# Attention with a gated mixer on one core: shifted keys copied within SBUF instead of computed by products

## The chip, the cores and the metric

The kernel runs on one core of a Trainium2 chip. The metric is the device time of one execution in microseconds, as a median of several runs. The profile is one further execution, taken by the hardware profiler; its span, and all times within it, count from the first instruction.

## What is computed

The input `x` is 2048 tokens by 512, in bf16. Path A is attention with 32 query heads of width 16 that share one head of keys and values. Path B is a gated MLP whose gate mixes along the tokens. A sigmoid per token mixes the two.

```python
g = sigmoid((x * gate_w).sum(-1))
q = (x @ wq) as 32 heads of 16;  k = x @ wk;  v = x @ wv
a = softmax(q k^T / 4) v, heads joined, @ wo
z = gelu(x @ w_in)            # 2048 x 1376
z1, z2 = halves of z;  z2 = layernorm(z2)
b = (z1 * (w_sp @ z2 + b_sp)) @ w_out
out = g * a + (1 - g) * b
```

## The kernel before

**Units.** The attention is cut into 32 units: a chunk of 512 queries (4 of them) times 4 heads (8 groups of them). A unit needs its scores against 16 tiles of 128 keys, for each of the 4 heads: 64 blocks of 128 keys by 512 queries. A score block is one product of the TensorE (PE) with 32 contracted rows: `ps<-QA,KA` in the rows of the trace. The 4 heads of a unit take the 4 groups of 32 rows. A group holds two heads of 16 rows, so that two units share one query tile `QA`: the even unit multiplies by keys that stand in rows 0 to 15 of each group with zeros below (`KA[:,0,:]`, "K0"), the odd unit by the same keys in rows 16 to 31 with zeros above (`KA[:,1,:]`, "K1", the shifted keys).

**Two ways to the exponential.** Most blocks go to the ScalarE (ACT): one activation for 2 blocks (1024 columns), sometimes 3 (1536) or 1 (512), writes `P` (line L770). The others go to the VectorE (DVE) in batches of 4 blocks (one key tile): a linear step from PSUM into `UW` (L782), a square (L789) and a second square (L795, of which GpSimd (POOL) takes a part). The products with the values, `ps<-P,V`, `ps<-UW,V` and `ps<-UW,VW`, and two small ones of sums (`ps<-QA,KTV`, `ps<-CT,SVB`) end the unit.

**Fillers.** Between these the PE does the products of path B, of queries and of the output projections. Everything on the PE but score blocks goes through the helper at L354.

**The planner.** The order is not written out. While the kernel is built, a planner keeps a clock for PE, ACT and DVE with a modelled cost per instruction, and emits the next instruction of the engine that is free first. How many batches the DVE gets, and how many blocks an activation takes, follow from it. Its constants stand at the head of the file: `A_OV` is the modelled fixed cost of an activation, `FLEX` bounds the DVE's backlog below which the third bank of an activation step goes to the DVE, `WARM` counts the products of a constant tile `CT` ahead of all others (L353). When the PE would idle after 20 us of planned time, it emits **zero products** (`ps<-CT,zer`) that add zeros or write an unused bank.

**The head.** The transposed loads of `x` come in four chunks of 512 tokens in the order 0, 3, 2, 1 (`XO`, on SyncE's (SP's) queue). For each chunk the PE makes K0 (`g_K`: 4 contraction steps of 4 products, 16 rows `ps<-xT,wk_rep`), then V (`ps<-wvg,xT`). The DVE evacuates K0 into `KA` (L426). After V of the last chunk come the products of **K1**, again 16 per chunk, from a second copy of the weights placed in the tile `z1` (`ps<-xT,z` in the rows, where buffer numbers are left out), and again a DVE evacuation at L426. A batch of an odd unit needs K1 of chunk 3. SP's queue goes on in order: `win` (L297), `bspz`, `wo`, `wout`, then `wT`.

**The end.** After the last unit the DVE normalizes and transposes in two halves (L807 to L838); 16 products `ps<-wo,OT` finish four output tiles of 128 tokens, numbers 12 to 15. The DVE evacuates 12 and 13 (L697), ACT 15 and 14 (L728). SP stores 12, 13 and 14, ACT stores 15.

Of the kernel before, what the change touches and what calls it, by code (L numbers as in the profile page):

```python
# [7 lines left out]
ALU = mybir.AluOpType  # L8
# [8 lines left out]
DH = 16  # L17
# [4 lines left out]
NU = 32  # L22
# [18 lines left out]
NZ = 22  # L41
WARM = 12
RLAST = 16
XO = (0, 3, 2, 1)
N0 = 3
A_OV = 63.3
HEAD = 45000.0
# [8 lines left out]
W_GEL = 0.98  # L56
PR = dict(HALF=100.0, IDR=10, IDN=4, WRES=16, D_HG=2500.0, D_FL=False, WIN=1000.0, WIH=560.0, BACK=32, PRESS=5, FLEX=5000.0, RMIN=32, WBL=0.5, W_MIN=0.9, HOLD=0.0, RLEND=0)
SCHED = {}
# [108 lines left out]
def build_kernel(nc, x_d, wq_d, wk_d, wv_d, wo_d, win_d, wsp_d, bsp_d, wout_d, gw_d, out_d):  # L167
    es = ExitStack()
    with es:
# [75 lines left out]
        SF = tmp[:, 64 * NMAX:96 * NMAX].rearrange("p (k w) -> p k w", w=32)  # L245
        wk_r = [wk_rep[:], z1f[:, 512 * NZ - 512:512 * NZ].rearrange("p (a n) -> p a n", a=4)]
        PT = z2[:, 0:2048].bitcast(F32).rearrange("p (a n) -> p a n", a=2)
# [6 lines left out]
        op("dve", lambda v: v.memset(CT[:], 1.0 / 64.0), w=["CT"])  # L254
        for e in range(2):
            op("dve", lambda v, e=e: v.memset(wk_r[e], 0.0), w=[("wk_rep", e)])
# [37 lines left out]
        op("act", lambda q: q.dma_start(wvg[:, :, 0:DH], wv_d.rearrange("(dt p) d -> p dt d", p=128)), w=["wv"], dma=16)  # L294
        op("act", nonc(lambda q: q.dma_start(wvg[:, :, 2 * DH:2 * DH + 1], gw_d.rearrange("(dt p one) -> p dt one", p=128, one=1))), w=["gw"], dma=16)
        def ld_win():
# [21 lines left out]
        def ld_rest():  # L318
            ld_bsp(0)
            sp_dma(ld_wo, w=["wo"], n=128)  # L320
# [5 lines left out]
        for e in range(2):  # L326
            op("dve", lambda v, e=e: v.tensor_scalar(wk_r[e].rearrange("p a (g e d) -> p a g e d", e=2, d=DH)[:, :, :, e, :],
                                                     wk_sb[:].unsqueeze(2).broadcast_to([128, 4, 4, DH]), 0.25, None, ALU.mult),
               r=["wk"], w=[("wk_rep", e)])

# [30 lines left out]

        ld_win()
        ld_rest()
        for _ in range(WARM):
# [53 lines left out]

        def g_K(c, lo=0, hi=512, e=0, b=BM):
            key = "K0a" if c == XO[0] and lo == 0 and e == 0 else ("K%d" % e, c)  # L420

            def piece(dt):
                return lambda: fm(b, hi - lo, 0, wk_r[e][:, dt, :], xT[:, dt, 512 * c + lo:512 * c + hi], dt == 0, dt == 3, [("wk_rep", e), ("x", c), ("z1", 5)], "K")

            def ev():
                op("dve", lambda v: v.tensor_copy(KA[:, e, 512 * c + lo:512 * c + hi], bank(b, hi - lo)), r=[bkey(b)], w=[key], tag="Kev")  # L426

            def done(t):
                T[key] = t
                if e == 0 and all(("K0", c2) in T for c2 in range(4)) and hi == 512:  # L430
# [465 lines left out]
        for i, c in enumerate(XO):  # L896
# [5 lines left out]
        first = deque([g_K(XO[0], 0, 128), g_Q(0, DBK[0]), g_K(XO[0], 128, 512), g_V(XO[0], BO), g_K(XO[1]), g_V(XO[1], BO), g_K(XO[2]), g_V(XO[2]),  # L902
                       g_K(XO[3]), g_V(XO[3])] + [g_K(c, e=1) for c in (XO[1], XO[0], XO[2], XO[3])])
        early = deque()
# [12 lines left out]
        tails = deque([g_part(12), g_part(13), g_flag(),  # L917
                       g_out(14, BM, None, True, "sp"),
                       g_out(15, DBK[0], lambda: d_done(), True, "act"),
                       g_fin(12, EB[0][0], lambda: when(("Bend", 0)), "sp"),  # L920
# [315 lines left out]
        pbusy = deque()  # L1236
        pidle = [0]

        def pe_step(now):
            r = pe_work(now)  # L1240
            if r is None:
# [3 lines left out]
                u = st_["pu"]  # L1245
                if now > 20000.0 and b < (W_GEL if gst["arm"] and gst["t"] > now - 8000.0 else pr["W_MIN"]) * W_WIN:
                    lim, topen = limit(now)
# [464 lines left out]
        if INFO is not None:  # L1712
            print({"end": last_end, "busy": busy, "batches": len(batches), "hist": hist, "left": left, "sbuf": nc.sbuf_bytes_remaining})
            print("warm", pidle[0])
            INFO.update(T=T, units=units, estart=estart, stepb=stepb, busy=busy, log=log)
        if INFO is not None and st_["pu"] < NU:
# [177 lines left out]
```

## Time and profile before

| what | value |
|---|---|
| median of 3 runs | 729.82 us (729.63 to 729.87) |
| the profiled execution, its own time | 732.05 us |
| its span | 730.2 us |
| granted TensorE clock, mean of the span | 0.993 |
| busy: PE, DVE, ACT, POOL | 714.8, 704.5, 711.9, 466.9 us |
| exponentials on ACT | 741 |
| score blocks that go through the DVE | 552 |

A row of a timeline has start and duration in us, engine, line, operation, tiles out<-in, shapes and the count; in square brackets how long the engine sat idle ahead of it, and what ended that. A row of the stretches has the busy time of PE, weight loads, DVE, ACT and POOL, then the granted clock of the PE (1.00 is full speed), the share of the DMA engines, and GB/s. A row of the groups by shape has the count, the busy time in us, the mean ns of one, and the idle time ahead of them. A row of the waits has who waited for whom, us in total, times, and the longest. A row of the DMAs ends in the us from issue to landing.

### The profile page before, as it was taken

To read this page: it belongs to the slowest core of one execution; us is meant where nothing else is said; L and a number is where in the kernel's file an instruction comes from. 1 tells how busy PE (TensorE), PEld (TensorE's weight loads), DVE (VectorE), ACT (ScalarE), POOL (GpSimd) and SP (SyncE) were. 2 spreads that over 40 slices of the span, in tenths; PEclk is the share of its full clock that TensorE was granted. 3 is DMA by queue.
4 is the path that set the end of the run, shared out by engine and by line. 5 is a ranking of instruction groups with operands and counts; after the bars stand their busy time and mean duration, and the time that the engine had idled before them with its cause. 6 is when DMAs were issued, how large, how long until landed. Compare 5 with 4: busy or idle time off the path is not lost.

```text
span 730.2 us, 21786 instructions
## 1 busy us (share of the span) xinstructions
PE 714.8 (98%) x9037; PEld 208.4 (29%) x9037; DVE 704.5 (96%) x1035; ACT 711.9 (98%) x760; POOL 466.9 (64%) x437
## 2 busy tenths in 40 slices
PE   8999999999999999999999999999999999999996
PEld 3322333323422223222222222222232222222321
DVE  5799999999999999999999999999999999999995
ACT  4999999999999999999999999999999999999996
POOL 5643666662166778776677777767776567667661
PEclk8999999999999999999999999999999999999999
DMA  8340000000000000500000051000005100000000
GB/s 189 110 108 10 2 1 2 2 3 2 2 2 1 2 2 2 116 24 9 1 2 2 3 103 36 10 2 1 3 2 105 27 10 9 1 3 2 2 2 33
DMA packets 48608, 17.28 MB, mean 24 GB/s; under 512 B 44180, under 2 KB 47992, under 8 KB 48504
## 3 DMA queue, kind: packets, MB, share of 16 engines
q1 hardware_dynamic: 46248, 15.54, 9.4%
q8 instruction: 72, 1.18, 0.6%
q10 hardware_dynamic: 2256, 0.30, 0.3%
q14 instruction: 32, 0.26, 0.1%
HBM read 3.25 MB, written 2.10 MB: 7 GB/s over the span
## 4 chain that ended last, share of the span: by engine, by line
PE 69%; ACT 17%; DVE 9%; issue 5%; ACTq 0%; DVEq 0%
PE ps L354 69%; ACT P L770 15%; DVE UW L782 4%; DVE UW L789 1%; DVE UW L795 1%; PE ps L353 1%; ACT z L1327 1%; DVE z L584 1%; DVE bst L598 0%; ACT z L592 0%; DVE T L807 0%; DVE km L453 0%; DVE KA L426 0%; DVE QA L471 0%; ACT outsb L728 0%
## 5 line engine op out<-in xcount | busy, mean ns | idle before, releaser
L770 ACT ACTIVATE P<-ps 128x1024 bf16<-128x1024 f32 (+1 forms) x741 | 686.6, 1177 | 7.8 <-PE ps L354 7.5
L795 POOL TENSOR_TENSOR UW<-UW 128x512 f16<-128x512 f16 (+1 forms) x281 | 363.5, 1294 | 161.2 <-DVE UW L795 67.4
L782 DVE TENSOR_SCALAR UW<-ps 128x512 f16<-128x512 f32 (+1 forms) x424 | 347.0, 840 | 4.1 <-PE ps L354 3.1
L354 PE MATMUL ps<-QA,KA 32*128 32x512 bf16 x2048 | 312.8, 386 | 6.1 <-ACT P L770 2.9
L354 PE MATMUL ps<-P,V 128*32 128x512 bf16 x1496 | 212.9, 387 | 0.3 <-DVE KN L499 0.2
L354 PEld LDWEIGHTS ps<-QA,KA 32*128 32x128 bf16 x2048 | 84.5, 91 | 309.7 <-ACT P L770 152.8
L789 DVE TENSOR_TENSOR UW<-UW 128x2048 f16<-128x2048 f16 (+1 forms) x163 | 171.8, 1056 | 0.6
L354 PE MATMUL ps<-UW,VW 128*32 128x512 f16 x552 | 118.9, 384 | 0.0
L354 PE MATMUL ps<-wT,z 128*32 128x512 bf16 (+1 forms) x1536 | 116.2, 366 | 0.0
L795 DVE TENSOR_TENSOR UW<-UW 128x1024 f16<-128x1024 f16 (+5 forms) x167 | 108.4, 664 | 0.2
L354 PE MATMUL ps<-UW,V 128*32 128x512 f16 x552 | 84.4, 384 | 0.2 <-DVE T L807 0.2
L354 PEld LDWEIGHTS ps<-P,V 128*32 128x32 bf16 x1496 | 49.0, 94 | 57.0 <-issue 51.1
L475 POOL TENSOR_TENSOR QSQ<-QA 128x512 bf16<-128x512 bf16 x16 | 28.9, 1806 | 22.9 <-DVE z L612 7.0
L354 PEld LDWEIGHTS ps<-wT,z 128*32 128x32 bf16 x1536 | 27.7, 94 | 42.5 <-issue 41.9
L354 PEld LDWEIGHTS ps<-UW,VW 128*32 128x32 bf16 x552 | 28.1, 94 | 15.0 <-issue 11.6
L354 PE MATMUL ps<-wout,z 128*32 128x512 bf16 x384 | 31.6, 384 | 0.0
L354 PE MATMUL ps<-win,xT 128*32 128x344 bf16 x512 | 30.8, 312 | 0.1
L830 POOL TENSOR_TENSOR Tn<-T,rc 128x512 bf16<-128x512 f32 x15 | 24.6, 1638 | 6.4 <-DVE UW L782 3.1
L807 DVE STREAM_TRANSPOSE T<-ps 128x512 f32<-128x512 f32 (+1 forms) x33 | 22.7, 691 | 4.1 <-PE ps L354 4.1
L354 PE MATMUL ps<-QA,KTV 128*32 128x512 bf16 x128 | 25.0, 384 | 0.0
L354 PE MATMUL ps<-CT,SVB 128*32 128x512 bf16 x128 | 24.6, 384 | 0.0
L354 PEld LDWEIGHTS ps<-UW,V 128*32 128x32 bf16 x552 | 20.0, 94 | 15.6 <-issue 11.3
(116 smaller groups left out, 380.1 us busy)
## 6 DMA issues: line engine op xcount, KB each, us to landing
out_dram<-outsb SPq DMA_DIRECT2D x15, 128.0 KB, 1.7
win<-in_B_w_in_dram SPq DMA_DIRECT2D x1, 1376.0 KB, 6.0
wout<-in_B_w_out_dram SPq DMA_DIRECT2D x1, 640.0 KB, 4.8
wo<-in_A_wo_dram SPq DMA_DIRECT2D x8, 64.0 KB, 2.3
UW<-in_A_wq_dram SPq DMA_DIRECT2D x1, 384.0 KB, 4.0
wT<-in_B_w_sp_dram SPq DMA_TRANSPOSE x16, 4.6
UW<-in_A_wq_dram ACTq DMA_DIRECT2D x1, 128.0 KB, 3.9
out_dram<-outsb ACTq DMA_DIRECT2D x1, 128.0 KB, 2.7
```

The costliest lines, as they stand in the source:

```text
L353: return t.matmul(dst, lhsT, rhs, start=start, stop=stop)
L354: return t.matmul(dst, lhsT, rhs, start=start, stop=stop, tile_position=tp)
L475: dq(pl_q, 1050.0, lambda: op("pool", lambda v: v.tensor_tensor(QSQ[:, q % 2, :], QA[:, q % NQ, :], QA[:, q % NQ, :], ALU.mult), r=[("Q", ...
L584: ev = lambda: op("dve", lambda v: v.tensor_copy(z2[:, FH * st + 344 * h:FH * st + 344 * h + 344], bank(BM, 344)), r=[bkey(BM)], w=[("z2", ...
L770: op("act", lambda a: a.activation(P[:, 512 * p0:512 * (p0 + n)], ps[:, 512 * b0:512 * (b0 + n)], ACT.Exp), r=[bkey(b0 + i_) for i_ in ran ...
L782: op("dve", lambda v: v.tensor_scalar(UW[:, 0, s, 512 * i:512 * (i + n)], bank(b, 512 * n), Q_A, Q_AS, ALU.mult, ALU.add), r=[bkey(b + j) ...
L789: op("dve", lambda v: v.tensor_tensor(src, src, src, ALU.mult), r=k, w=k, tag="dTT")
L795: op(eng, lambda v: v.tensor_tensor(UW[:, 1, s, 256 * a:256 * b], src, src, ALU.mult), r=[("U", s, h) for h in range(a // 2, (b + 1) // 2) ...
L807: return lambda: pgx.op("dve", lambda v: v.transpose(T1[:, jj, c0:c1], bank(BO, c1 - c0, c0)), r=[bkey(BO)], w=[("T1", jj, c0)], tag="T1")
L830: pgx.op(eng, lambda v: v.tensor_tensor(tnv[:, pr, j0:j1, b0:b1, :], t1v[:, j0:j1, b0:b1, 0:16], rc[:, j0:j1, b0:b1].unsqueeze(3).broadcas ...
L1327: op("act", lambda a: a.activation(z1f[:, 512 * i0:512 * (i0 + n)], ps[:, 512 * b0:512 * (b0 + n)], ACT.Gelu_apprx_tanh), r=[bkey(b0 + j) ...
```

## The change

The products and evacuations of K1 go, with the second copy of the weights. Instead SP copies, per chunk, rows 0 to 111 of K0 into rows 16 to 127 of K1: 112 rows of 1 KB, once the chunk's K0 is evacuated. The zeros that this leaves out (rows 0 to 15 of the first group) are written by POOL at the start. On SP's queue the copies of chunks 3, 0 and 2 stand ahead of `win`, that of chunk 1 ahead of `bspz` and what follows. `WARM` goes from 12 to 11. After the last product of the last unit the planner emits zero products for 1850 ns. Tile 14 is stored by ACT, tile 15 by SP. `A_OV` and `FLEX` are lower. `W_HEAD` has the value that stood in the code before, and the factor 1.0 beside it is for planned times below 20 us, which that value excludes.

```diff
-WARM = 12
+WARM = 11
+W_HEAD = 20000.0
+W_TAIL = 1850.0
-A_OV = 63.3
+A_OV = 62.9
-PR = dict(... FLEX=5000.0 ...)
+PR = dict(... FLEX=3500.0 ...)
+op("pool", lambda g: g.memset(KA[0:32, 1, :], 0.0), w=[("K1", c) for c in range(4)])
+def ld_K1(c, t):
+    op("sp", lambda q: q.dma_start(KA[16:128, 1, 512*c:512*c+512], KA[0:112, 0, 512*c:512*c+512]),
+       r=[("K0", c)] + (["K0a"] if c == XO[0] else []), w=[("K1", c)], dma=16, tag="K1")
+    spc["free"] = max(spc["free"], t) + 650.0
+    T[("K1", c)] = spc["free"] + 2300.0
 # in g_K, when the evacuation of chunk c is planned:
+if hi == 512 and c == XO[1]:
+    ld_K1(c, t)
+    ld_K1(XO[0], t)
+elif hi == 512 and c == XO[2]:
+    ld_K1(c, t)
+    ld_win()
+elif hi == 512 and c == XO[3]:
+    ld_K1(c, t)
+    ld_bsp(0)
+    sp_dma(ld_wo, w=["wo"], n=128)
+    ld_rest()
-first = deque([...] + [g_K(c, e=1) for c in (XO[1], XO[0], XO[2], XO[3])])
+first = deque([...])
-g_out(14, BM, None, True, "sp"), g_out(15, DBK[0], lambda: d_done(), True, "act"),
+g_out(14, BM, None, True, "act"), g_out(15, DBK[0], lambda: d_done(), True, "sp"),
 # in pe_step, when the PE has nothing to do:
+if u >= NU and tend[0] is not None and now + C_V <= tend[0] + W_TAIL:
+    fm(EB[1][0] + 1, 512, 0, zer[:], CT[:], True, True, ["zer", "CT"], "warm")
-elif now > 20000.0 and b < (W_GEL if ... else pr["W_MIN"]) * W_WIN:
+elif now > W_HEAD and b < (1.0 if now < 20000.0 else W_GEL if ... else pr["W_MIN"]) * W_WIN:
```

**What moves on SP, at the head of its queue.** Before, `win` follows the loads of `x`:

```order
L287 DMA_TRANSPOSE xT<-in_A_x_dram 128x4x512 x2
L291 DMA UW<-in_A_wq_dram 128x4x384
L287 DMA_TRANSPOSE xT<-in_A_x_dram 128x4x512 x2
L297 DMA win<-in_B_w_in_dram 128x4x1376
L300 DMA bspz<-in_B_b_sp_dram 1x512
L306 DMA wo<-in_A_wo_dram 16x4x512 x8
```

With the change the four copies stand among them:

```order
L288 DMA_TRANSPOSE xT<-in_A_x_dram 128x4x512 x2
L292 DMA UW<-in_A_wq_dram 128x4x384
L288 DMA_TRANSPOSE xT<-in_A_x_dram 128x4x512 x2
L300 DMA KA<-KA 112x512 x3
L306 DMA win<-in_B_w_in_dram 128x4x1376
L300 DMA KA<-KA 112x512
L309 DMA bspz<-in_B_b_sp_dram 1x512
L315 DMA wo<-in_A_wo_dram 16x4x512 x8
```

So `win` now waits on this queue for K0 of the third chunk, and all that follows for K0 of the fourth.

**What moves on the DVE, around the evacuation of the fourth chunk's K0** (the first `KA` row of each piece). Before, from the evacuation of the sums to the third evacuation of K1:

```order
L550 TENSOR_SCALAR z<-ps 128x512
L795 TENSOR_TENSOR UW<-UW 128x1024 x2
L426 CAST KA<-ps 128x512
L492 CAST V<-ps 128x4x16
L495 TENSOR_SCALAR gs<-ps 128x4
L570 TENSOR_SCALAR G<-E 128x16
L571 RECIPROCAL G<-G 128x16
L426 CAST KA<-ps 128x512
L782 TENSOR_SCALAR UW<-ps 128x512
L426 CAST KA<-ps 128x512
L782 TENSOR_SCALAR UW<-ps 128x512 x2
```

With the change, from the same place:

```order
L565 TENSOR_SCALAR z<-ps 128x512
L797 TENSOR_SCALAR UW<-ps 128x1024
L810 TENSOR_TENSOR UW<-UW 128x1024 x2
L797 TENSOR_SCALAR UW<-ps 128x512
L430 CAST KA<-ps 128x512
L797 TENSOR_SCALAR UW<-ps 128x512 x2
L804 TENSOR_TENSOR UW<-UW 128x2048
L507 CAST V<-ps 128x4x16
L510 TENSOR_SCALAR gs<-ps 128x4
L797 TENSOR_SCALAR UW<-ps 128x1024
L585 TENSOR_SCALAR G<-E 128x16
L586 RECIPROCAL G<-G 128x16
```

The work on batches of the odd unit 1 (`UW` rows) now stands ahead of and around the last evacuation of K0, where before the DVE had only small evacuations. Over the whole program ACT gets 738 exponentials with 1492 blocks, where it had 741 with 1496: 718 of 1024 columns (725 before), 18 of 1536 (15), 2 of 512 (1). The DVE gets 139 batches, where it had 138. Ahead of path B's gelu, ACT now has 332 blocks in 163 exponentials (347 in 171 before), behind it 1160 in 575 (1149 in 570); the DVE has 115 blocks ahead of it and 441 behind (116 and 436).

**What moves on ACT and the PE at the end.** ACT before, from its last exponentials on:

```order
L770 ACTIVATE P<-ps 128x1536
L770 ACTIVATE P<-ps 128x1024 x2
L728 ACTIVATE outsb<-ps,G 128x512
L662 DMA out_dram<-outsb 128x512
L728 ACTIVATE outsb<-ps,G 128x512
```

With the change:

```order
L785 ACTIVATE P<-ps 128x1024
L785 ACTIVATE P<-ps 128x1536
L785 ACTIVATE P<-ps 128x1024
L743 ACTIVATE outsb<-ps,G 128x512 x2
L677 DMA out_dram<-outsb 128x512
```

The PE before, from the last unit's sums on:

```order
L354 MATMUL ps<-QA,KTV 32x512 x4
L354 MATMUL ps<-P,V 32x512 x2
L354 MATMUL ps<-CT,SVB 32x512 x4
L354 MATMUL ps<-UW,VW 32x512 x4
L354 MATMUL ps<-P,V 32x512 x2
L354 MATMUL ps<-wo,OT 32x512 x16
```

With the change:

```order
L360 MATMUL ps<-QA,KTV 32x512 x4
L360 MATMUL ps<-CT,SVB 32x512 x4
L360 MATMUL ps<-P,V 32x512 x2
L360 MATMUL ps<-CT,zer 32x512 x32
L360 MATMUL ps<-wo,OT 32x512 x16
```

ACT's two evacuations now follow each other, with its store behind both, and 32 zero products stand between the last unit and the output projection.

More of the change, by code (lines that the diff above doesn't have):

```diff
@@ L56 @@
 W_GEL = 0.98
[L57 removed]
+PR = dict(HALF=100.0, IDR=10, IDN=4, WRES=16, D_HG=2500.0, D_FL=False, WIN=1000.0, WIH=560.0, BACK=32, PRESS=5, FLEX=3500.0, RMIN=32, WBL=0.5, W_MIN=0.9, HOLD=0.0, RLEND=0)
 SCHED = {}
@@ L254, in build_kernel @@
         op("dve", lambda v: v.memset(CT[:], 1.0 / 64.0), w=["CT"])
-        for e in range(2):
-            op("dve", lambda v, e=e: v.memset(wk_r[e], 0.0), w=[("wk_rep", e)])
+        op("dve", lambda v: v.memset(wk_rep[:], 0.0), w=["wk_rep"])
         op("dve", lambda v: v.memset(V1[:], 0.0), w=[("V", c) for c in range(4)])
@@ L324, in ld_rest @@
             ld_wT(0)
[L326 to L329, printed above, removed]
+        op("dve", lambda v: v.tensor_scalar(wk_rep[:].rearrange("p a (g e d) -> p a g e d", e=2, d=DH)[:, :, :, 0, :],
+                                            wk_sb[:].unsqueeze(2).broadcast_to([128, 4, 4, DH]), 0.25, None, ALU.mult),
+           r=["wk"], w=["wk_rep"])
         def wq_tile(eng, t, key, raw):
@@ L417, in qt, with g_K @@
             return 1e12 if t is None else t
-        def g_K(c, lo=0, hi=512, e=0, b=BM):
-            key = "K0a" if c == XO[0] and lo == 0 and e == 0 else ("K%d" % e, c)
+        def g_K(c, lo=0, hi=512, b=BM):
+            key = "K0a" if c == XO[0] and lo == 0 else ("K0", c)
             def piece(dt):
-                return lambda: fm(b, hi - lo, 0, wk_r[e][:, dt, :], xT[:, dt, 512 * c + lo:512 * c + hi], dt == 0, dt == 3, [("wk_rep", e), ("x", c), ("z1", 5)], "K")
+                return lambda: fm(b, hi - lo, 0, wk_rep[:, dt, :], xT[:, dt, 512 * c + lo:512 * c + hi], dt == 0, dt == 3, ["wk_rep", ("x", c)], "K")
             def ev():
-                op("dve", lambda v: v.tensor_copy(KA[:, e, 512 * c + lo:512 * c + hi], bank(b, hi - lo)), r=[bkey(b)], w=[key], tag="Kev")
+                op("dve", lambda v: v.tensor_copy(KA[:, 0, 512 * c + lo:512 * c + hi], bank(b, hi - lo)), r=[bkey(b)], w=[key], tag="Kev")
             def done(t):
                 T[key] = t
-                if e == 0 and all(("K0", c2) in T for c2 in range(4)) and hi == 512:
+                if hi == 512 and c == XO[1]:
[9 more added lines that the diff above has]
+                    ld_rest()
+                if all(("K0", c2) in T for c2 in range(4)) and hi == 512:
                     for c2 in range(4):
@@ L902, in build_kernel @@
         first = deque([g_K(XO[0], 0, 128), g_Q(0, DBK[0]), g_K(XO[0], 128, 512), g_V(XO[0], BO), g_K(XO[1]), g_V(XO[1], BO), g_K(XO[2]), g_V(XO[2]),
-                       g_K(XO[3]), g_V(XO[3])] + [g_K(c, e=1) for c in (XO[1], XO[0], XO[2], XO[3])])
+                       g_K(XO[3]), g_V(XO[3])])
         early = deque()
@@ L1152, in pv_emit @@
                 st_["pu"] += 1
+                if st_["pu"] == NU:
+                    tend[0] = t_end
                 unit_end(pu, t_end + L_PE)
@@ L1237, in build_kernel @@
         pidle = [0]
+        tend = [None]
         def pe_step(now):
@@ L1245, in pe_step @@
                 u = st_["pu"]
-                if now > 20000.0 and b < (W_GEL if gst["arm"] and gst["t"] > now - 8000.0 else pr["W_MIN"]) * W_WIN:
+                if u >= NU and tend[0] is not None and now + C_V <= tend[0] + W_TAIL:
+                    fm(EB[1][0] + 1, 512, 0, zer[:], CT[:], True, True, ["zer", "CT"], "warm")
+                    pidle[0] += 1
+                    r = now + C_V
+                elif now > W_HEAD and b < (1.0 if now < 20000.0 else W_GEL if gst["arm"] and gst["t"] > now - 8000.0 else pr["W_MIN"]) * W_WIN:
                     lim, topen = limit(now)
@@ L1714, in build_kernel @@
             print("warm", pidle[0])
-            INFO.update(T=T, units=units, estart=estart, stepb=stepb, busy=busy, log=log)
+            INFO.update(pg=pg, T=T, units=units, estart=estart, stepb=stepb, busy=busy, log=log)
         if INFO is not None and st_["pu"] < NU:
```

11 lines of the change are left out of this document (4 added, 7 removed).

## The prediction

> **What bounds the kernel now.** I read the busy times first, then stretches of the span, then ACT's waits.
>
> ```profile
> PE 714.8 (98%) x9037; PEld 208.4 (29%) x9037; DVE 704.5 (96%) x1035; ACT 711.9 (98%) x760; POOL 466.9 (64%) x437
> ```
>
> Three engines are nearly full, so the average doesn't name the bound. The stretches do: from the head's end to the gelu, from behind the gelu to the end of the attention, and the tail.
>
> ```profile
> 9.70:21.00 11.30, 10.29 (x197) 2.79 (x190) 6.46 (x14) 9.46 (x10) 6.09 (x13) 0.70 0.83 204
> 21.00:171.00 150.00, 146.78 (x1957) 45.45 (x1949) 145.82 (x205) 149.87 (x163) 94.29 (x100) 1.00 0.10 25
> 195.00:720.00 525.00, 523.38 (x6344) 144.84 (x6334) 520.59 (x728) 524.59 (x569) 360.94 (x301) 1.00 0.08 17
> 720.00:730.20 10.20, 3.20 (x43) 0.87 (x38) 3.71 (x12) 3.18 (x4) 0.00 (x0) 0.86 0.17 57
> ```
>
> ACT (fourth busy time) idles 0.13 of 150 us and 0.41 of 525 us; the DVE (third) 4.2 and 4.4. In the whole span ACT waits for the PE's scores for 7.5 us, of which 5.5 are the start:
>
> ```profile
> ACT P L770 <- PE ps L354: 7.5, 6, 5.5
> ```
>
> So the time is ACT's work, plus the head, plus the tail. The DVE binds as strongly only if work is moved to it without room. The room lies in the head:
>
> ```profile
> 20.00:40.00 20.00, 19.92 (x406) 7.04 (x402) 15.39 (x30) 19.51 (x21) 15.32 (x35) 0.98 0.30 82
> ```
>
> 4.6 us of DVE idle time stand here, most of them where it has no batch because unit 1's keys are not there:
>
> ```profile
> 27.95 0.69 DVE L426 CAST KA<-ps 128x512 bf16<-128x512 f32 x1 [0.68 <-PE ps L354]
> ...
> 31.54 0.69 DVE L426 CAST KA<-ps 128x512 bf16<-128x512 f32 x1 [0.95 <-PE ps L354]
> 33.26 0.69 DVE L782 TENSOR_SCALAR UW<-ps 128x512 f16<-128x512 f32 x1 [1.02 <-PE ps L354]
> ```
>
> The last K0 is evacuated at 27.95, the first K1 at 31.54, and the first batch of unit 1 begins at 33.26.
>
> **Part 1: K1 by copy, and the batch that it pays for: -1.9 us.** ACT's price of a block and of an instruction:
>
> ```profile
> L770 ACT ACTIVATE P<-ps 128x1024 bf16<-128x1024 f32 x725 | 668.0, 1171 | 2.0 <-PE ps L354 1.7
> ...
> L1327 ACT ACTIVATE z<-ps 128x1536 bf16<-128x1536 f32 x3 | 4.3, 1447 | 0.2 <-PE ps L354 0.2
> L1327 ACT ACTIVATE z<-ps 128x1024 bf16<-128x1024 f32 x4 | 4.1, 1016 | 0.1
> ```
>
> One of 1024 columns costs 668.0/725 = 0.921 us of ACT's time (its own 1171 ns overlap with the next); 512 columns more cost 1.447 - 1.016 = 0.431. The order gives 7 fewer of 1024, 3 more of 1536 (1.352) and 1 more of 512 (0.490): -6.45 + 4.06 + 0.49 = **-1.9 us**. I take all of it, since ACT has no idle time in which to lose it unnoticed.
>
> It holds only if the DVE carries its side.
>
> ```profile
> L782 DVE TENSOR_SCALAR UW<-ps 128x512 f16<-128x512 f32 x296 | 191.6, 678 | 3.6 <-PE ps L354 3.0
> L782 DVE TENSOR_SCALAR UW<-ps 128x1024 f16<-128x1024 f32 x128 | 155.4, 1214 | 0.5 <-PE ps L354 0.2
> L789 DVE TENSOR_TENSOR UW<-UW 128x2048 f16<-128x2048 f16 x113 | 138.1, 1222 | 0.6
> L795 DVE TENSOR_TENSOR UW<-UW 128x1024 f16<-128x1024 f16 x113 | 76.3, 685 | 0.1
> ```
>
> Linear steps: 14 more of 1024 (1.21), 24 fewer of 512 (0.65): +1.5. Squares: the order holds 4608 columns more in 9 more instructions; from 1.22 for 2048 and 0.68 for 1024 a column costs 0.53 ns and an instruction 0.13 us: +3.6. Four evacuations of 0.69 go: -2.8 (the second copy of the weights goes too, unpriced). Sum +2.3, where the span is to shrink by 2.4: 4.7 of the DVE's 25.7 idle us (730.2 - 704.5) must go, and unit 1's batches now stand where the 4.6 above lie.
>
> The split at the gelu agrees: ahead of it ACT has 15 blocks in 8 instructions fewer (at 0.43, and the 0.06 that 0.921 leaves for an instruction: -6.9 us), behind it 11 in 5 more (+5.0). The gelu's table load should move from 171.6 to near 164.5:
>
> ```profile
> 171.56 1.28 ACT L592 ACT_TABLE_LOAD   x1
> ```
>
> The copy itself must not be late. Chunk 3's waits for the evacuation at 12.10; like transfers land after about 2 us:
>
> ```profile
> 12.10 0.69 DVE L426 CAST KA<-ps 128x512 bf16<-128x512 f32 x1 [1.94 <-PE ps L354]
> ```
> ```profile
> wo<-in_A_wo_dram SPq DMA_DIRECT2D x8, 64.0 KB, 2.3
> ```
>
> So it lands at 12.8 + 2.3 = 15.1 us, or near 19 if it takes as long as `win`, 6.0 (below). The order has unit 1's first score (a 3 in place of a 2) here:
>
> ```profile
> 22.76 0.39 PE L354 MATMUL ps<-QA,KA 32*128 32x512 bf16 x2
> ```
>
> The cover is 7.7 us, so I cost the copy at nothing. Later than 22.76, it would hold the PE, and all scores for ACT queued behind it.
>
> Behind it on SP, `win` is held until K0 of chunk 2 stands, at 19.4, and lands 6 us later, near 26; its first reader on the PE stands behind the last K0 (evacuated at 27.95), V and a query tile. The weights behind the fourth copy wait for that evacuation and are read after the gelu. POOL's zeros lie ahead of a gap of 5.03 us in which it waits for `wq`, and cost nothing up to that:
>
> ```profile
> 18.72 0.69 DVE L426 CAST KA<-ps 128x512 bf16<-128x512 f32 x1 [0.38 <-PE ps L354]
> ```
> ```profile
> win<-in_B_w_in_dram SPq DMA_DIRECT2D x1, 1376.0 KB, 6.0
> ```
> ```profile
> 9.79 1.32 POOL L333 COPY wqd<-UW 128x256 bf16<-128x256 bf16 x3 [5.03 <-DMA UW<-in_A_wq_dram]
> ```
>
> The PE loses 64 products (16 groups of four at 0.22 us, 3.5 us) which were covered by ACT; that gives nothing by itself.
>
> **Part 2: one warm product fewer: -0.2 us.**
>
> ```profile
> 1.44 5.30 PE L353 MATMUL ps<-CT 128*128 128x512 bf16 x12 [1.44 <-DVE CT L254]
> 6.67 0.59 PE L354 MATMUL ps<-xT,wk_rep 128*32 128x128 bf16 x16
> 7.07 1.06 PE L354 MATMUL ps<-xT,wqd 128*32 128x512 bf16 x16
> ```
> ```profile
> 0.72 4.96 SPq L287 DMA_TRANSPOSE xT<-in_A_x_dram  x2
> ```
> ```profile
> xT<-in_A_x_dram SPq DMA_TRANSPOSE x1, 5.2
> ```
>
> The first load of `x` is issued at 0.72 and lands at 5.9; the first K0 starts at 6.67, right behind the 12 products of 0.43 us each. One fewer frees 0.43 us. But these are half-speed products (0.43, where groups of four from 7.07 on take 0.22). If full speed comes at the same instant, the query products start in the slow part and give back about half. Bounds 0 and -0.43; I take -0.2.
>
> **Part 3: the end: -0.3 us.**
>
> ```profile
> 725.21 0.69 ACT L728 ACTIVATE outsb<-ps,G 128x512 bf16<-128x512 f32 x1 [3.40 <-PE ps L354]
> 725.93 0.37 ACTq L662 DMA_DIRECT2D out_dram<-outsb  x1
> 726.40 0.69 ACT L728 ACTIVATE outsb<-ps,G 128x512 bf16<-128x512 f32 x1 [0.50 <-ACT outsb L728]
> ```
> ```profile
> 727.11 0.42 SPq L662 DMA_DIRECT2D out_dram<-outsb  x1
> ```
> ```profile
> out_dram<-outsb SPq DMA_DIRECT2D x1, 128.0 KB, 2.4
> ```
> ```profile
> out_dram<-outsb ACTq DMA_DIRECT2D x1, 128.0 KB, 2.7
> ```
>
> ACT's store sits between its two evacuations. Without it the second starts at 725.9, and the last store is issued at 726.6, not 727.11. It lands 2.4 to 2.7 us later: -0.2 to -0.5. I take -0.3, nearer to ACT's own 2.7. The zero products (8 groups, 1.8 us) fall into the PE's wait here:
>
> ```profile
> 724.32 1.05 PE L354 MATMUL ps<-wo,OT 128*32 128x512 bf16 x16 [2.07 <-DVE OT L838]
> ```
>
> 1.8 is less than 2.07, and the 16 products already run at 0.22 a group, so they gain and cost nothing. The cover has 0.3 us to spare; what it falls short of would be added to the end.
>
> **Sum.** -1.9 - 0.2 - 0.3 = -2.4 us. The profiled execution took 732.05 (span 730.2 and 1.85 around it), 2.2 above the median; the difference carries over: 732.05 to 729.65, or 729.82 to **727.4 us**.
>
> **Rivals.**
> *The DVE doesn't keep up ahead of the gelu.* There ACT's time falls by 6.9 us, and the DVE's work by 3.5 (the four evacuations, and one block at about 0.7): it must do with 3.4 us less idle time, most of what it has from 20 to 40. If the idle time stays, the batch's 1.9 go and only 0.5 remain: 729.3. For it: no reserve. Against: DVE work now stands in those gaps.
>
> *The new order feeds ACT later, slower than before.* 23 exponentials take 21.18 us in a quiet stretch, which is (21.18 - 1.17)/22 = 0.909 each; the mean of all is 0.921. So 12 ns each are waits for scores. The mechanism is the PE's order behind the gelu, where other things now stand ahead of the scores. If these waits double, that is 738 x 0.012 = 8.9 us: 736.3. It eats the gain from 3 ns each on, and is slower than before by more than 0.2% from 5 ns on. Against: behind the gelu ACT and DVE both have 11 and 5 blocks more, at the mix of before.
>
> ```profile
> 59.61 21.18 ACT L770 ACTIVATE P<-ps 128x1024 bf16<-128x1024 f32 x23
> ```
>
> *The half-speed stretch goes away.* Inside the stretch from 9.7 to 21 us, with its mean of 0.70, the PE falls to half clock (the granted clock stands ahead of the last two numbers):
>
> ```profile
> 14.00:15.00 1.00, 1.00 (x9) 0.10 (x2) 0.97 (x2) 1.00 (x2) 0.89 (x3) 0.50 0.21 44
> ```
>
> ACT idles 1.84 of 11.3 us there (9.46 busy). The head now runs 0.2 us earlier, which packs more work ahead of the drop. If the drop then fails to come, 1.8 more are won: 725.6. Against: the order up to 22 us is the same.
> The Trainium skill, TensorE: Matmul & The Clock Gate, "Part 1: The HAM clock gate", says the clock falls after at least one idle window of about 3.4 us. By that rule there would be no drop here to lose, and the sum stays 727.4; the trace disagrees, since the PE was busy 10.29 of 11.30 us and still fell to half.
>
> *The change doesn't do what it says*, the copies being unused until later: the DVE's order excludes it.
>
> **How the numbers follow.** Forecast 0.64 (own range 726.4 to 728.8), DVE short of room 0.20, slower 0.08, half-speed gone 0.08. A measurement of this kernel can tell about 0.2%, 1.46 us, from no change. Faster: 0.08 and most of the forecast, 0.56; same: 0.20 and the rest, 0.08; slower 0.08. The range takes in 725.6 and 729.3 with some margin for the sizes: 725.5 to 729.9.
>
> **What will show it.** Right: 738 exponentials; ACT idle under 1 us between 21 us and the end of attention; DVE busy over 18.5 us from 20 to 40; the table load near 164.5; the copies landing by 17 us; the first K0 near 6.3 us; the last store at a distance of 1.4 us, not 1.9, from ACT's first evacuation. Wrong: DVE gaps ended by the PE ahead of the gelu, a mean exponential over 0.924, or PE rows waiting for `KA`'s copies.

## The result, and the profile after

The changed kernel takes **731.68 us** (median of 9 runs, 731.53 to 732.5), the kernel before 729.94 beside it (9 runs): a ratio of 1.0023, with a 95% interval of 1.0012 to 1.0033. It is slower by 1.7 us, where 2.4 us less were forecast.

One thing about the ground of the comparison: the stretch at half clock in the first profile of before (14 to 20.8 us) is missing in most executions (of the nine of before, eight take 729.63 to 730.25 us and one, like that profile, 732.06), so from here on before is read in a second profile, with a span of 727.9 us, and after in one of 730.0. The gap to close is thus **+2.1 us** of span.

The busy times of after:

```profile
PE 709.3 (97%) x9004; PEld 207.4 (28%) x9004; DVE 711.0 (97%) x1028; ACT 710.7 (97%) x757; POOL 471.9 (65%) x439
```

DVE rose by 6.5 us, where the sum had 2.3. The stretches say where it matters; second profile of before first (busy PE, weight loads, DVE, ACT, POOL, then the clock), then after:

```profile
14.00:15.00 1.00, 0.64 (x9) 0.10 (x2) 0.97 (x2) 1.00 (x3) 0.89 (x3) 1.00 0.95 213
20.00:40.00 20.00, 19.91 (x351) 6.62 (x349) 16.16 (x27) 20.00 (x22) 16.85 (x38) 1.00 0.33 97
40.00:60.00 20.00, 19.06 (x210) 5.28 (x208) 20.00 (x25) 19.87 (x22) 6.15 (x6) 1.00 0.43 93
```
```profile
20.00:40.00 20.00, 18.61 (x330) 6.26 (x323) 19.96 (x29) 18.95 (x23) 16.98 (x38) 1.00 0.40 135
40.00:60.00 20.00, 18.47 (x217) 5.25 (x217) 20.00 (x25) 18.52 (x20) 6.92 (x6) 1.00 0.39 86
21.00:171.00 150.00, 144.60 (x1929) 45.67 (x1926) 148.41 (x203) 147.45 (x157) 89.46 (x96) 1.00 0.12 33
```

Before, ACT was busy 39.87 of these 40 us; after, 37.47. The PE, too, has less to do. The DVE's row says 19.96 of 20 while the other two starve. ACT's waits for scores, before (second profile) and after (in all these rows the scores, too, have the line of the helper, L354 and now L360):

```profile
ACT P L770 <- PE ps L354: 5.8, 2, 5.5
```
```profile
ACT P L785 <- PE ps L360: 8.3, 10, 5.3
```

Two waits became ten. Each costs more than its gap: from the start at 44.07 to that at 45.52 us (rows below) it is 1.45 us, 0.54 more than in a row, around a gap of 0.43. So I count the distance from one start to the next. Where nothing waits it is 0.904 to 0.921 us for 1024 columns and 1.330 to 1.348 for 1536; I take 0.908 and 1.335, and by the same step 0.48 for 512 columns, which no row shows in a run of them. What exceeds this I call **lost time**. Over all exponentials that start from 20 to 60 us it is 0.8 us before and 4.1 after. The span's +2.1 is then: the first exponential 0.2 earlier (9.74 to 9.54); ACT's smaller work -1.9 (the same distances, over the exponentials and evacuations of each trace); lost time from 20 to 60 us **+3.3**; lost time elsewhere and ACT's other work +0.6; and 0.3 more from the last exponential to the end (8.40 to 8.69).

What fills the DVE from 40 to 46 us of after; DVE, POOL, PE and ACT:

```profile
40.19 1.20 DVE L797 TENSOR_SCALAR UW<-ps 128x1024 f16<-128x1024 f32 x1
41.32 1.91 DVE L804 TENSOR_TENSOR UW<-UW 128x2048 f16<-128x2048 f16 x1
43.16 1.52 DVE L810 TENSOR_TENSOR UW<-UW 128x1024 f16<-128x1024 f16 x1
44.60 0.68 DVE L468 TENSOR_REDUCE km<-ps 128x1 f32<-128x512 f32 x1
45.20 1.21 DVE L797 TENSOR_SCALAR UW<-ps 128x1024 f16<-128x1024 f32 x1
```
```profile
41.11 1.04 POOL L490 TENSOR_TENSOR QSQ<-QA 128x512 bf16<-128x512 bf16 x1
42.94 1.19 POOL L452 TENSOR_TENSOR KSQ<-KA 128x512 bf16<-128x512 bf16 x1 [0.79 <-PE ps L360]
```
```profile
43.29 0.39 PE L360 MATMUL ps<-UW,V 128*32 128x512 f16 x1 [0.37 <-DVE UW L804]
...
46.47 0.40 PE L360 MATMUL ps<-QA,KA 32*128 32x512 bf16 x4 [0.47 <-DVE UW L797]
```
```profile
39.87 3.77 ACT L785 ACTIVATE P<-ps 128x1024 bf16<-128x1024 f32 x4
44.07 1.02 ACT L785 ACTIVATE P<-ps 128x1024 bf16<-128x1024 f32 x1 [0.43 <-PE ps L360]
45.52 1.02 ACT L785 ACTIVATE P<-ps 128x1024 bf16<-128x1024 f32 x1 [0.43 <-PE ps L360]
46.99 1.02 ACT L785 ACTIVATE P<-ps 128x1024 bf16<-128x1024 f32 x1 [0.45 <-PE ps L360]
```

Two squares last 1.91 and 1.52 us that elsewhere take 1.22 and 0.68. Each begins while POOL is at an instruction and ends a fixed time behind it: QSQ ends at 42.15, the square of 2048 columns at 43.23, 1.08 later; KSQ ends at 44.13, the square of 1024 at 44.68, 0.55 later. The linear step at 40.19, which reads PSUM, is not touched by POOL; of the 133 steps of 1024 columns in after that begin beside a POOL instruction, none lasts over 1.23 us. The step at 45.20, which frees a PSUM bank, is so much later; the PE's scores wait for that bank (46.47), and ACT for the scores. The Trainium skill, SBUF — State Buffer, "SBUF: two separate sides", says that VectorE and GpSimd share a pair of ports which one instruction holds to its end while the other is blocked, and that a VectorE operation with two SBUF inputs is among those concerned, against GpSimd work that reads SBUF. The trace agrees, with the 1.08 and 0.55 us above.

From 15 to 60 us seven squares of after are stretched like this, by 2.8 us together; in the second profile of before it is 0.6. Each of the seven ends 1.07 or 1.08 us (2048 columns) or 0.54 or 0.55 us (1024) behind the POOL instruction beside which it began. Over the whole span, squares by count and mean, before (second profile) and after:

```profile
L789 DVE TENSOR_TENSOR UW<-UW 128x2048 f16<-128x2048 f16 (+1 forms) x163 | 171.8, 1056 | 0.6
L795 DVE TENSOR_TENSOR UW<-UW 128x1024 f16<-128x1024 f16 (+5 forms) x167 | 108.4, 664 | 0.2
```
```profile
L804 DVE TENSOR_TENSOR UW<-UW 128x2048 f16<-128x2048 f16 (+1 forms) x166 | 174.4, 1052 | 1.1
L810 DVE TENSOR_TENSOR UW<-UW 128x1024 f16<-128x1024 f16 (+4 forms) x173 | 112.3, 660 | 0.2
```

Count times mean gives 172.1 + 110.9 = 283.0 before and 174.6 + 114.2 = 288.8 after: +5.8, where the working had 3.6. The 2.2 between them are the stretched squares of 15 to 60 us (2.8 less 0.6).

### The profile page after: what moved, and what is told of

It reads as the page before. It is cut to its first block, busy times and chain, and to the rows that moved or that the text cites. A ratio compares the mean times of both kernels' runs of the same rounds, so it can differ in the third digit from the quotient of the medians.

```text
span 730.0 us, 21704 instructions
## 1 busy us (share of the span) xinstructions
PE 709.3 (97%) x9004; PEld 207.4 (28%) x9004; DVE 711.0 (97%) x1028; ACT 710.7 (97%) x757; POOL 471.9 (65%) x439
## 4 chain that ended last, share of the span: by engine, by line
PE 59%; ACT 21%; DVE 11%; issue 7%; DMA 1%; ACTq 0%
PE ps L360 59%; ACT P L785 21%; DVE UW L797 4%; DVE bst L613 2%; DVE UW L810 2%; DVE UW L804 2%; DVE z L627 1%; DMA wvg<-in_gate_w_dram 1%; DVE T L822 0%; ACT z L607 0%; DVE mv L617 0%; DVE QA L486 0%; DVE Tn L845 0%; ACT L607 0%; DVE z L599 0%
## 5 line engine op out<-in xcount | busy, mean ns | idle before, releaser
L810 POOL TENSOR_TENSOR UW<-UW 128x512 f16<-128x512 f16 (+1 forms) x282 | 369.6, 1311 | 163.3 <-DVE UW L810 63.6
L360 PE MATMUL ps<-QA,KA 32*128 32x512 bf16 x2048 | 311.7, 384 | 10.1 <-ACT P L785 5.3
L360 PE MATMUL ps<-P,V 128*32 128x512 bf16 x1492 | 207.2, 385 | 0.2 <-DVE KN L514 0.2
L804 DVE TENSOR_TENSOR UW<-UW 128x2048 f16<-128x2048 f16 (+1 forms) x166 | 174.4, 1052 | 1.1
L360 PEld LDWEIGHTS ps<-QA,KA 32*128 32x128 bf16 x2048 | 83.8, 91 | 310.8 <-ACT P L785 159.3
L360 PE MATMUL ps<-UW,VW 128*32 128x512 f16 x556 | 117.5, 384 | 0.2 <-DVE UW L810 0.2
L360 PE MATMUL ps<-wT,z 128*32 128x512 bf16 (+1 forms) x1536 | 115.9, 366 | 0.0
L810 DVE TENSOR_TENSOR UW<-UW 128x1024 f16<-128x1024 f16 (+4 forms) x173 | 112.3, 660 | 0.2
L360 PE MATMUL ps<-UW,V 128*32 128x512 f16 x556 | 83.9, 384 | 1.2 <-DVE T L822 0.7
L360 PEld LDWEIGHTS ps<-P,V 128*32 128x32 bf16 x1492 | 47.7, 94 | 52.4 <-issue 48.5
L490 POOL TENSOR_TENSOR QSQ<-QA 128x512 bf16<-128x512 bf16 x16 | 26.4, 1648 | 23.2 <-DVE UW L797 10.5
L360 PEld LDWEIGHTS ps<-wT,z 128*32 128x32 bf16 x1536 | 28.8, 94 | 43.2 <-issue 41.8
L360 PEld LDWEIGHTS ps<-UW,VW 128*32 128x32 bf16 x556 | 27.8, 94 | 15.9 <-issue 11.9
L360 PE MATMUL ps<-wout,z 128*32 128x512 bf16 x384 | 31.8, 384 | 0.0
L360 PE MATMUL ps<-win,xT 128*32 128x344 bf16 x512 | 31.0, 312 | 0.7 <-DVE QA L486 0.7
L845 POOL TENSOR_TENSOR Tn<-T,rc 128x512 bf16<-128x512 f32 x15 | 22.9, 1526 | 8.0 <-DVE UW L797 4.0
L360 PEld LDWEIGHTS ps<-UW,V 128*32 128x32 bf16 x556 | 19.6, 94 | 18.4 <-issue 11.7
L360 PE MATMUL ps<-CT,SVB 128*32 128x512 bf16 x128 | 22.9, 384 | 0.0
L360 PE MATMUL ps<-xT,win 128*32 128x512 bf16 (+1 forms) x384 | 22.5, 363 | 0.2 <-ACT P L785 0.2
```

The lines of the kernel that those rows point to most:

```text
L360: return t.matmul(dst, lhsT, rhs, start=start, stop=stop, tile_position=tp)
L490: dq(pl_q, 1050.0, lambda: op("pool", lambda v: v.tensor_tensor(QSQ[:, q % 2, :], QA[:, q % NQ, :], QA[:, q % NQ, :], ALU.mult), r=[("Q", ...
L804: op("dve", lambda v: v.tensor_tensor(src, src, src, ALU.mult), r=k, w=k, tag="dTT")
L810: op(eng, lambda v: v.tensor_tensor(UW[:, 1, s, 256 * a:256 * b], src, src, ALU.mult), r=[("U", s, h) for h in range(a // 2, (b + 1) // 2) ...
L845: pgx.op(eng, lambda v: v.tensor_tensor(tnv[:, pr, j0:j1, b0:b1, :], t1v[:, j0:j1, b0:b1, 0:16], rc[:, j0:j1, b0:b1].unsqueeze(3).broadcas ...
```

## The experiments

The theories, as the expectations name them. **A**: the loss sits where the copies put unit 1's batches, from 20 to 60 us. **B**: it sits in the planner's new constants. Within A, **A1**: the squares wait beside POOL's instructions, and ACT starves for it; **A2**: the DVE simply has too much to do there, or the first key blocks of chunk 1 are late. A further rival to A1: the PE waits for POOL's late results.

### The kernel before, once more

No edit.

> The kernel before, unchanged, profiled once more. Theory 1 (the profile shown was one with the half-speed stretch, while most executions have none): the granted clock stays 1.00 from 10 to 21 us, ACT idles under 0.5 us there instead of 1.84, and the profiled execution takes about 729.9 us instead of 732.05, with all else as in the first profile. Rival (the stretch belongs to every execution, and 732.05 is what a profile adds): the stretch is there again and the time is 732 us.

729.73 us (one execution), span 727.9; the granted clock is 1.00 from 14 to 15 us (row above), and ACT is busy 20.00 us of 20 to 40. The half-clock stretch, one of whose rows carried a rival, is no part of the usual execution, and what the change could win by its going away was never there.

### The end and the warm products alone

Before, with:

```diff
-WARM = 12
+WARM = 11
+W_TAIL = 1850.0        # and the zero products of the end
-g_out(14, ..., "sp"), g_out(15, ..., "act")
+g_out(14, ..., "act"), g_out(15, ..., "sp")
```

> The kernel before with only the edits at its two ends: 11 warm products, zero products after the last unit, tile 14 stored by ACT and 15 by SP. K1 by products, old constants, so the plan between is that of before. My sum gives -0.2 for the start and -0.3 for the end, 729.4 us; the trace of the changed kernel (first exponential at 9.54 instead of 9.74, last store issued 1.3 us behind ACT's first evacuation) gives up to -0.7. A rival in which the ends cause the loss gives 731.5.

729.97 us against 729.84, ratio 1.0000 (0.9991 to 1.0009). The first exponential starts 0.07 us earlier. The end, before (second profile) and here, ACT and SP's queue:

```profile
722.94 0.69 ACT L728 ACTIVATE outsb<-ps,G 128x512 bf16<-128x512 f32 x1 [3.41 <-PE ps L354]
...
724.12 0.69 ACT L728 ACTIVATE outsb<-ps,G 128x512 bf16<-128x512 f32 x1 [0.50 <-ACT outsb L728]
```
```profile
723.28 2.38 SPq L662 DMA_DIRECT2D out_dram<-outsb  x3
```
```profile
722.87 1.27 ACT L729 ACTIVATE outsb<-ps,G 128x512 bf16<-128x512 f32 x2 [3.40 <-PE ps L355]
```
```profile
723.22 2.75 SPq L663 DMA_DIRECT2D out_dram<-outsb  x3
```

ACT's evacuations end at 724.14 instead of 724.81, as forecast. But SP's three stores are not through sooner: the issue of the last begins earlier and now takes 1.9 us instead of 0.8, and the three end at 725.97 instead of 725.66. The trace's landing times show what the end of that issue goes with: the first of the three stores lands at 726.48 before and at 726.68 here, and the third issue ends 0.8 and 0.7 us ahead of that. It is so, within 0.7 to 0.8 us, in 13 of the 14 traces of this case (0.3 in the other, where the second issue is the long one), whenever the third issue began. So an earlier third store only took longer to issue; no run tests what holds it. The 0.5 us that the two parts were to bring are not there.

### The copies with the old constants

After, with:

```diff
-A_OV = 62.9
+A_OV = 63.3
-PR = dict(... FLEX=3500.0 ...)
+PR = dict(... FLEX=5000.0 ...)
```

> The changed kernel with A_OV 63.3 and FLEX 5000 as before: the copies with the old constants. Theory A (the copies bring DVE work into the stretch from 20 to 45 us, where POOL is busy and the DVE's instructions get longer, and the PE waits behind late evacuations): still over 731 us, ACT's waits from 20 to 60 us over 2 us. Theory B (the new constants give a looser order everywhere): between 727.5 and 729.8 us, waits from 20 to 60 us under 1 us.

732.11 us, ratio 1.0035 (1.0022 to 1.0049); 4.0 us lost from 20 to 60 us. The loss comes without the new constants: B falls as the cause, A stands.

### The products with the new constants

Before, with `A_OV` 62.9, `FLEX` 3500 and the edits of the run on the end; K1 by products.

> K1 by products as before, with all else of the change: the new constants, 11 warm products, the new end. Theory A: no DVE work ahead of 33 us, no loss there, 729.0 to 729.6 us. Theory B: the loss stays, over 731 us.

731.09 us, ratio 1.0018 (1.001 to 1.0027), 0.9 us lost from 20 to 60 us. By its time this is what B had expected, and A's 729.0 to 729.6 is missed. But the place is not that of the changed kernel, and the plan offers another reason: its ACT has 1500 blocks where before has 1496, one batch less on the DVE, which at 0.43 us a block is 1.7 us. So the constants alone cost something too, as far as the trace shows by the plan that they lead to and not by ACT's waits from 20 to 60 us. It doesn't clear B's constants of harm in themselves; it shows that the harm in the changed kernel, which has 1492 blocks, is a different one.

### Without POOL's work of the head: after, and before

In both kernels:

```diff
+def op(eng, fn, tag="", **kw):
+    if eng == "pool":
+        nsq[0] += tag == "QSQ"
+        if tag in ("SF", "SVB", "KF", "KTV", "RT", "KSQ") or tag == "QSQ" and nsq[0] <= 3:
+            return None
+    return pg.op(eng, fn, tag=tag, **kw)
+# KSQ, QSQ and RT are filled with constants at the start
```

> The changed kernel without GpSimd's work of the head: the sums and copies of SF, SVB, KF and KTV, the sixteen RT copies, the four key squares and the first three query squares are left out (their tiles hold constants instead, so the output is not the reference's); every instruction of TensorE, VectorE, ScalarE and SyncE stands in the same order as in the changed kernel. Theory A1 (in 20 to 60 us VectorE's squares wait beside GpSimd's instructions, about 2.2 us in all, and ScalarE starves for it): the squares there go back to 0.68 and 1.22 us, VectorE's busy time in 20 to 40 us falls from 19.96 to about 18, ScalarE's waits of 20 to 60 us fall from 4.1 to under 1.5 us, and the time falls by 2 to 3 us, to 728.7 to 729.7. Theory A2 (VectorE has too much work in that place even alone, or the first key blocks of chunk 1 are late): the waits stay above 2.5 us and the time at 731 or more.

> The control to the run beside it: the kernel before without the same work of GpSimd (left out in the same way). ScalarE waits only 0.8 us there in 20 to 60 us and VectorE has 16.2 us of work in 20 to 40 us, so theory A1 has nothing to win here: under 0.7 us. Theory A2 expects the same. If this one gains as much as the run beside it, the loss of the change has nothing to do with GpSimd.

After without this work takes **728.38 us**, ratio 0.9973 (0.996 to 0.9985); before without it 729.83, 0.9995 (0.9984 to 1.0006). The same cut brings the changed kernel 3.3 us (731.68 to 728.38), and the kernel before 0.3, which its interval doesn't tell from nothing. The profiles of these two runs have the half-clock stretch again, from 14 to 20.8 us, ahead of the rows that are read here. No square from 15 to 60 us is stretched in either, and 0.8 us are lost by ACT from 20 to 60 us of the changed one, as many as before had. The place of above in the changed kernel, DVE and ACT:

```profile
40.99 1.21 DVE L808 TENSOR_SCALAR UW<-ps 128x1024 f16<-128x1024 f32 x1
42.12 1.21 DVE L815 TENSOR_TENSOR UW<-UW 128x2048 f16<-128x2048 f16 x1
43.25 0.68 DVE L821 TENSOR_TENSOR UW<-UW 128x1024 f16<-128x1024 f16 x1
43.85 0.69 DVE L479 TENSOR_REDUCE km<-ps 128x1 f32<-128x512 f32 x1
44.45 1.22 DVE L808 TENSOR_SCALAR UW<-ps 128x1024 f16<-128x1024 f32 x1
```
```profile
39.84 7.51 ACT L796 ACTIVATE P<-ps 128x1024 bf16<-128x1024 f32 x8
```

From one linear step to the next it is 3.46 us here and 5.01 in the changed kernel; the difference of 1.55 is the two stretched squares (0.70 + 0.84). ACT runs through. A1 is right, and its 3.3 us are a little more than the 2 to 3 expected; A2 falls, since the DVE's list of instructions is the same. The expectation that the DVE's busy time from 20 to 40 us would fall to 18 was wrong: it stays at 19.4.

### The same POOL work, read by nobody

After, with GpSimd's instructions in place but writing to a scratch tile:

```diff
-g.tensor_tensor(KSQ[:], KA..., KA...), w=["KSQ"]
+g.tensor_tensor(KSQ_, KA..., KA...), w=["SCR"]     # likewise QSQ (first three), SVB, KTV, RT
```

> The changed kernel with all of GpSimd's work of the head back, instruction for instruction and as long, but its results go to a scratch tile that nobody reads (the tiles that are read hold constants, so the output is not the reference's); the other engines' instructions stand in the same order. If the 3.3 us that the run without GpSimd's work won were the squares that wait beside its instructions (theory A1), all of it comes back: squares of 25 to 53 us stretched by 2.2 to 2.8 us in sum, ScalarE's waits of 20 to 60 us 3.5 to 4.3 us, time 731.2 to 732.2. If it was TensorE waiting for GpSimd's results (late key squares, sums or ratios), the time stays at 728.2 to 729.

**732.31 us**, ratio 1.003 (1.0018 to 1.0041): all of it is back, 0.1 above the expected range, with 3.2 us of stretched squares and 4.0 us lost from 20 to 60 us. Nobody reads what POOL makes in the head, so the PE cannot be waiting for it; POOL's being at work is enough. DVE and POOL at the same place:

```profile
41.59 1.91 DVE L814 TENSOR_TENSOR UW<-UW 128x2048 f16<-128x2048 f16 x1
43.43 1.52 DVE L820 TENSOR_TENSOR UW<-UW 128x1024 f16<-128x1024 f16 x1
```
```profile
41.38 1.04 POOL L500 TENSOR_TENSOR z<-QA 128x512 bf16<-128x512 bf16 x1
42.50 1.90 POOL L462 TENSOR_TENSOR z<-KA 128x512 bf16<-128x512 bf16 x1
```

The rows also show the wait the other way round. POOL's second square starts at 42.50, in the midst of the DVE's, which ends at 43.50, and lasts 1.90 instead of 1.04: to 44.40, 0.9 behind the DVE's end.

### The copies, but no early batch

After, with the plan told that K1 is there at 32.2 us, and `A_OV` 63.3 (ACT then has 1496 blocks, as before):

```diff
-T[("K1", c)] = spc["free"] + 2300.0
+T[("K1", c)] = max(spc["free"] + 2300.0, 32200.0)
```

> The changed kernel with the copies as they are, but the plan told that the shifted keys are there only at 32.2 us, and A_OV 63.3; ScalarE's plan then has 738 exponentials over 1496 blocks, the block count of before. Theory A (the loss is the early batch's squares, not the copies as transfers or the weights loaded behind them): ScalarE's waits of 20 to 60 us are near those of before, 0.8 to 1.5 us, and the time is 729.5 to 730.3. Rival: the copies themselves, or the later weights, cost; then the waits stay at 2.5 to 4 us and the time at 731.5 to 732.5.

730.37 us against 730.10, ratio 1.0001 (0.9992 to 1.001); 0.95 us lost from 20 to 60 us.

```profile
20.00:60.00 40.00, 38.92 (x594) 12.54 (x591) 34.30 (x48) 39.68 (x43) 22.39 (x43) 1.00 0.44 114
```

ACT is busy 39.68 of 40 us with all four copies running and the weights behind them. The copies as transfers cost nothing that can be seen; the early batches do.

### The plan told of the wait

The planner already adds POOL's remaining time to a square's cost for POOL's later work, but not for the head's. After, with that mended up to a bound, once with `H_LOCK` 300 and `FLEX` 5000, once with 200, `A_OV` 62.3 and `FLEX` 3500:

```diff
+hlock = []
 def pool_t(cost, t=0.0):
     plc["free"] = max(plc["free"], clk["now"], t) + cost
+    hlock.append((plc["free"] - cost, plc["free"]))
     ...
 def lock(now):
-    return max(0.0, plc["lock"] - now)
+    h = max([min(H_LOCK, y - now) for x, y in hlock if x <= now < y] or [0.0])
+    return max(0.0, plc["lock"] - now, h)
```

> The changed kernel, whose plan is told that a square begun while GpSimd works on the head's sums, gate or squares takes up to 300 ns longer (H_LOCK 300, FLEX 5000); the plan has 1492 blocks, as the changed one. Theory A1: the batches then stand where they fit, ScalarE's waits of 20 to 60 us fall under 2.2 us and the time is 728.5 to 730; under the rival (the plan's place of the batches does not matter) it stays at 731.3 to 732.

> The same with up to 200 ns, A_OV 62.3 and FLEX 3500, again 1492 blocks: theory A1 728.5 to 730.3 with waits of 20 to 60 us under 2.5 us; rival 731.3 to 732.

732.17 us, 1.0026 (1.0016 to 1.0036), and 732.61, 1.0045 (1.0027 to 1.0063). Both times miss. With 200 the lost time from 20 to 60 us only falls to 2.4 us; its six executions spread from 731.85 to 735.77, and why it isn't faster than the changed kernel stays open. With 300 it falls to 0.6, as wanted, and the last exponential ends at 718.35 us instead of 721.26, but from there to the end it is 12.0 us instead of 8.7. ACT's last and the DVE's last work of that kernel:

```profile
715.88 2.48 ACT L788 ACTIVATE P<-ps 128x1024 bf16<-128x1024 f32 x2
```
```profile
719.37 0.69 DVE L800 TENSOR_SCALAR UW<-ps 128x512 f16<-128x512 f32 x1 [0.97 <-PE ps L361]
720.10 0.69 DVE L807 TENSOR_TENSOR UW<-UW 128x1024 f16<-128x1024 f16 x1
720.83 0.69 DVE L813 TENSOR_TENSOR UW<-UW 128x1024 f16<-128x1024 f16 x1
```

A block of the last batch reaches the DVE 1 us after ACT's end and is squared twice before the unit can close. The 2.9 us won at the start are lost at the end, in a place that has nothing to do with POOL.

### The plan told, and the end mended

After, with `H_LOCK` 300, `A_OV` 62.3, `FLEX` 3500, and `RLAST` 12 instead of 16 (how many blocks must be left in the last unit for the DVE still to get one); again 1492 blocks. And the same with the stores in the order of before.

> The changed kernel, its plan told of 300 ns for a square beside GpSimd's head work (H_LOCK 300), with A_OV 62.3, FLEX 3500 and RLAST 12, so that the last batch doesn't end behind ScalarE as it did in the first kernel of this kind; 734 exponentials over 1492 blocks. Theory A1: ScalarE's waits of 20 to 60 us under 1.5 us, the tail behind the last exponential 8.4 to 9 us, and the time 727.3 to 728.8, faster than both kernels. If the copies cost something beside the squares' waits, or if the waits come back elsewhere, 729.5 or more.

> The kernel beside it with the two last evacuations and their stores in the order of before (tile 14 on SyncE, tile 15 on ScalarE). From the run of the end alone (same time as before, with a tail 0.3 us longer by the profile): 0 to 0.4 us faster than the kernel beside it. If the new order gained what was forecast, it is 0.3 us slower.

**728.36 us** against 729.98, ratio 0.9981 (0.9972 to 0.9989): 0.2% faster than before, and faster than the changed kernel. The other 728.20, 0.9977 (0.9968 to 0.9987); the 0.16 between them lies inside the intervals, so the order of the stores stays undecided at this size.

```profile
20.00:60.00 40.00, 38.76 (x570) 12.22 (x563) 39.15 (x59) 39.82 (x44) 24.19 (x43) 1.00 0.41 110
```

ACT is busy 39.82 of 40 us in the first of the two, though some squares are still stretched (1.6 us). From the last exponential to the end it is 9.3 us, a little over the 8.4 to 9 expected. The DVE carries almost what it carries in the changed kernel, but not where it makes ACT wait. Since three constants were set anew with it, this run doesn't show by itself which of them brought how much.

## Why the prediction was wrong, point by point

**Part 1, ACT's side: right.** The trace has the 738 exponentials, ACT's own work is 1.9 us smaller, and with POOL out of the way the kernel gains 1.7 us (728.38 against 730.10; 1.5 against the kernel before without the same work), close to what the batch was to pay.

**Part 1, the DVE's side: the step that failed.** The +3.6 for the squares rests on 1.22 and 0.68 us, which are means over the whole span, and a wait of the squares beside POOL is put at nothing without a reason. At the place to which the batches move, POOL is busy 16.98 of 20 us, and a square that begins beside it lasts up to 1.91 and 1.52: +5.8 for the squares, and 3.3 us lost by ACT, more than the batch's 1.9. (Of the 4.2 us by which the DVE's busy time exceeds the forecast +2.3, these are 2.2; the rest isn't traced here.) The remark "I take all of it, since ACT has no idle time in which to lose it unnoticed" looked at ACT's idle time where it should have asked who frees ACT's banks. The quoted row of 20 to 40 us held POOL's 15.32 us of work, and nothing was asked of it.

**The copies, and SP's queue: right.** The first lands at 14.93 us, where 15.1 was worked out, and no product of the PE waits for one; the run without the early batch finds no cost. The sign "landing by 17 us" was stated too widely: the other three, each behind its K0, land at 17.09, 19.96 and 30.38.

```profile
KA<-KA SPq DMA_DIRECT2D x4, 112.0 KB, 2.3
```

**The table load: 165.51 us, not 164.5.**

```profile
165.51 1.28 ACT L607 ACT_TABLE_LOAD   x1
```

From 169.30 in the second profile of before, the forecast shift of 7 us would give 162.3; it came 3.2 later, the lost time of 20 to 60 us.

**Part 2: about right.** The first K0 starts at 5.85 us instead of 6.67, now held by the load of `x`; the first exponential comes 0.2 us earlier in the changed kernel, as forecast, but 0.07 in the run of the end and the warm product alone. Over the eleven traces with 11 warm products it starts at 9.23 to 9.67 us (mean 9.46), in the three with 12 at 9.74 to 9.77: about 0.3 is won, and a single trace can't tell 0.2 from it.

```profile
5.85 0.41 PE L360 MATMUL ps<-xT,wk_rep 128*32 128x128 bf16 x16 [0.20 <-DMA xT<-in_A_x_dram]
```

**Part 3: wrong.** ACT's side came as worked out, and the last issue begins 1.2 us behind ACT's first evacuation, as the sign wanted. But the sum let it take its usual time, and it grew from 0.8 to 1.8 us (1.9 in the run of the end alone), up to 0.8 us ahead of the first store's landing; the end is 0.3 us longer instead of 0.3 shorter.

**The sum.** "The difference carries over" did no harm: the 2.2 us between profile and median were the half-clock stretch, and each term was a difference.

**The signs.** "DVE busy over 18.5 us from 20 to 40" came true (19.96) and told nothing: 1.0 us of it is waiting beside POOL, since a blocked square counts as busy, but without POOL's work of the head the DVE is as full there (19.13 of 19.20 us from 20.8 to 40), and ACT runs through. The signs of the other side were there, too: a mean exponential of 664.0/718 = 0.925 us, over 0.924, and ACT idle 2.55 us from 21 to 171 alone.

**The rivals.** "The DVE doesn't keep up ahead of the gelu" named the right engine and stretch, but let the loss end at the batch's own 1.9 us; it was 3.3. "The new order feeds ACT later" had the side but another place: behind the gelu nothing of that size is lost. The half-clock rival was no possibility in the usual execution.

**Open** is what holds the last store's issue on SP until shortly before the first store lands, and what of the 1.6 us that the version with the plan told gains is due to each of its constants.

## What to carry to other kernels

Where work is moved to an engine's idle time, price it by the rows of that place, with what the neighbours do there, not by its mean over the span. A long mean on one engine beside a busy neighbour, which shrinks when the neighbour is taken away and returns when it works for nobody, is a wait on a shared resource; the busy column doesn't show it as one. And a planner that knows such a wait in one place must know it everywhere, or it will fill the very stretch that looks empty in its model.

## What the runs showed of the hardware

- A DVE square of two SBUF tensors that begins beside a POOL instruction ended 0.54 to 0.55 us (1024 columns) or 1.07 to 1.08 us (2048) behind POOL's end in all seven cases from 15 to 60 us of after in which it was stretched, whatever its own start; alone it takes 0.68 and 1.22. POOL's square of 512 columns, begun beside a DVE square, takes 1.90 instead of 1.04 and ends 0.9 behind it. The DVE's steps from PSUM (1.20) are not touched. Not every POOL instruction does this: beside POOL's `rstd` step of 2.94 us at 186 us of after, squares took 0.68 and 1.22.
- Three stores on SP's queue are issued within 2.38 us when the last one's data come 0.67 us later, and within 2.75 when they come at once: the third issue then takes 1.9 us instead of 0.8, and ends 0.7 to 0.8 us ahead of the first store's landing either way.
- The TensorE clock falls to half from 14 to 20.8 us in one profile and not in another of the same kernel (730.2 and 727.9 us of span).
